# Expert 0's first layers: routing items, slot writes, turns, gate copies and zero blocks placed anew

## Chip, cores and metric

One core of a Trainium2 chip. The metric is the device time of one execution in microseconds (us), as the median of several runs. Its engines have a queue each and run side by side: TensorE (PE: matrix products and transposes into PSUM), VectorE (DVE), ScalarE (ACT), GpSimd (POOL) and SyncE (SP, which issues DMA transfers).

## What is computed

A sliding-window attention over 8 batches of 576 positions (8 heads of 64), whose 4608 output rows of 512 go through a layer of 8 experts. A noisy gate picks two experts for each row:

```python
logits = x @ w_gate
noise_scale = np.log1p(np.exp(x @ w_noise))
noisy_logits = logits + noise_scale * noise
top2 = np.argpartition(-noisy_logits, 2, axis=1)[:, :2]
...
for e in range(E):
    for k in range(2):
        mask = top2[:, k] == e
        h = np.maximum(x[mask] @ w1[e], 0.0)
        out[mask] += top2_w[mask, k, None] * (h @ w2[e])
```

## The kernel before

**Attention.** A loop over j = 0 to 38 handles one block of 128 rows per step: scores(j), softmax, transposition of the probabilities, product with the values (pv, two steps later), normalisation (three steps later), store of the rows to DRAM (`X`). Every part is issued by hand at a fixed place of the step, so each engine's order of work is the order of the program. The scores of block j use one PSUM tile `ps_s` of two banks, the transposes one bank `ps_t`; one bank `ps_g` (`idle`, `G`) is shared by the gate logits (`VG`), the ranks and the slot sums (`SP`).

**Routing.** The 36 blocks are routed in five portions that end at j = 7, 14, 21, 27 and 36 (`ROUTE`). `route(c)` is a generator of some 45 small operations of DVE and ACT (noise, top two, running counts, then after a pause of six calls, `HOLD`, a rank by two small matmuls, then weights and positions). `drain(n)` issues the next n of them. At its end `route` appends the **slot steps** of its portion to the list `slots`: for each pair of blocks `at_tile` (DVE), `at_lane` (four comparisons with `lane`, on POOL in the loop and on DVE after it), `at_both` (POOL) and `place` (four bfloat16 matmuls into `SP`, and a DVE addition into `SLOT`). `drain_slots(n)` issues the next n. The lists of rows that each expert handles are made from `SLOT`.

**Expert 0 starts early.** Its rows are handled in three chunks of 384, 384 and 448. The first two hold only rows of the blocks before 14 and 27 (`EARLY`), so they don't need the last portion of the routing; the third does. Per chunk c: `gather(0, c)` fetches rows by an indirect DMA on POOL into `xg` (four buffers, used by `down` for its results too); a **gate copy** on DVE takes each tile's weights; `turn_first(c)` transposes them (f: four PE transposes; g: an ACT copy and a DVE subtraction, the high and the low part); `up_first(c)` has 32 steps, f = 0 to 7 by k = 0 to 3, of three matmuls each, and after k = 3 an eviction (ACT L818, DVE L819); `down_first(c)` has 24 or 32 steps, three or four tiles q by f = 0 to 7, an ACT copy into `xg` and a scattered addition to the output (`add_rows`, L929 on POOL). Sixteen steps of up(0, 0) are issued in the steps j = 36 to 38 of the loop (`ahead`), the other sixteen (f = 4 to 7) after it. I write up00, down00, up01, down01, up02 for the stages, f5k2 for a step of an up, q1f3 for one of a down.

**Side work.** `spread(main, total, *parts)` issues the items of each part between the steps of a stage; a part (a, b, items) lies evenly over the shares a to b of it. Beside up00 and down00 lie: the split of w2 into high and low parts (`split_w2`, ACT L242 and DVE L234), the fifth portion of the routing, its slot steps, the turns of the next chunk, and `zero_out`, 38 transfers of 256 KB on SP's queue that clear the output before anything is added to it. `catch_up` makes sure that chunk 1's gather has been issued. `settle` and a `drain_slots` of everything stand in up01 ahead of the list of the third chunk (`first_list(2)`) and its gather.

Of the kernel before, what the change touches and what calls it, by code (L numbers as in the profile page):

```python
# [8 lines left out]
F32 = mybir.dt.float32  # L9
F32R = mybir.dt.float32r  # L10
BF = mybir.dt.bfloat16
# [3 lines left out]
OP = mybir.AluOpType  # L15
# [23 lines left out]
TURN = 33  # L39
# [7 lines left out]
ZFROM, ZEACH, ZUP = 32, 3, 8  # L47
# [40 lines left out]
def tile_kernel(ctx, tc, qT, kT, vx, vT, wgx, noise, w1, w2, out):  # L88
# [336 lines left out]
    lane = consts.tile([128, 128], F32)  # L425
# [73 lines left out]
    def route(c):  # L499
# [20 lines left out]
        d, ra = new("d"), new("ra")  # L520
# [6 lines left out]
        y = new("y")  # L527
# [3 lines left out]
        for c2 in range(2):  # L531
            t, r1 = new("t1"), new("r1", [128, n])
            yield lambda: nc.vector.tensor_reduce(mm[:, c2], y, op=OP.max, axis=AX.X)
            yield lambda: nc.vector.tensor_tensor(t, y, bc(mm[:, c2]), op=OP.is_ge)
            yield lambda: nc.vector.tensor_tensor(t, t, rev[:, None, :].to_broadcast(sh), op=OP.mult)
            yield lambda: nc.vector.tensor_reduce(r1, t, op=OP.max, axis=AX.X)
            yield lambda: nc.vector.tensor_tensor(oh[:, c2], t, bc(r1), op=OP.is_equal)
            if c2 == 0:
                yield lambda: nc.vector.copy_predicated(y, oh[:, 0].bitcast(U32),
                                                        low[:, :n * E].rearrange("p (a b) -> p a b", a=n))  # L540
# [44 lines left out]
        def at_lane(q, x):  # L585
            if x == 0:
                AB[q] = piece("ha", [128, 4, 128], BF, 2), piece("hb", [128, 4, 2, E * NQ], BF, 2)
            for k in range(2):
                (nc.gpsimd if j < NT else nc.vector).tensor_scalar(AB[q][0][:, 2 * x + k], lane, lo[:, q + x, k:k + 1], None, op0=OP.is_equal)
# [20 lines left out]
        last = None  # L610
        for q in range(0, n, 2):
            m = min(2, n - q)
            slots.append(lambda q=q, m=m: (at_tile(q, m), at_lane(q, 0)))
            slots.append(lambda q=q, m=m: m > 1 and at_lane(q, 1))
            slots.append(lambda q=q, m=m, f=last: (f and f(), at_both(q, m)))
            last = lambda q=q, m=m: place(q, m)
        slots.extend([lambda: None, last])
# [49 lines left out]
    GW = {}  # L667
    seen = {(0, c): j for c, j in enumerate(sorted(EARLY))}

    def gather(e, c):  # L670
# [9 lines left out]
        if e == 0:  # L680
            return [lambda q=q, m=m: whole(q, m) for q, m in tiles(e, c)] + [lambda: None] * 2 + [
                lambda q=q, m=m: gate_of(q, m) for q, m in tiles(e, c)]
# [17 lines left out]
    def turn_first(c):  # L700
# [7 lines left out]
        def f(q, m):  # L708
            y = cur[q] = turn_bank()[:, :KD * m].rearrange("p (k m) -> p k m", k=KD)
            for k in range(KD):  # L710
                nc.tensor.transpose(y[:, k], XG[0, c, q][:m, k * 128:k * 128 + 128], ident[:m, :m])

# [80 lines left out]
    def up_first(c):  # L793
# [5 lines left out]
        for f in (0, 4, 1, 5, 2, 6, 3, 7) if tail else range(KF):  # L799
# [11 lines left out]
            for k in range(KD):  # L811
                nc.tensor.matmul(p[:, :n], lhsT=w1h[:, k, fs], rhs=xh[:, k, :n], start=(k == 0), stop=False)
                nc.tensor.matmul(p[:, :n], lhsT=w1h[:, k, fs], rhs=xl[:, k, :n], start=False, stop=False)
                nc.tensor.matmul(p[:, :n], lhsT=w1l[:, k, fs], rhs=xh[:, k, :n], start=False, stop=(k == KD - 1))
                if k < KD - 1:
                    yield
            h, l, t = (x[f] for x in HH[e, c])
            nc.scalar.activation(h, p[:, :main], AF.Relu)  # L818
            nc.vector.scalar_tensor_tensor(l, p[:, :main], 0.0, h.bitcast(F32), op0=OP.max, op1=OP.subtract)  # L819
# [241 lines left out]
    for j in range(NT + 3):  # L1061
# [46 lines left out]
        drain_slots(2 if j >= DENSE else 1 + j % 2)  # L1108
# [18 lines left out]
    for n, (e, c) in enumerate(work):  # L1127
# [3 lines left out]
        if n == 0:  # L1131
            for w in split_w2():
                side += [lambda: (drain(3), drain_slots(1))] * 2 + [w]

            def catch_up():
                while (0, 1, 2) not in XG:
                    drain(1)
                    drain_slots(1)
        elif n == 1:
            pending.append(count())  # L1140
            side += [lambda: (drain(6), drain_slots(1))] * 12
            side += [settle, lambda: drain_slots(10 ** 6), lambda: [x() for x in first_list(2)], lambda: None]
        elif c == 0:
            parts.append((0.55, 1.0, split_w2()))
        if nxt and n:
            rows_of = gather(*nxt)
            if n < 2:
                side += rows_of + [lambda: None] * 2
            else:
                parts.append((0.0, 0.65, rows_of))  # L1150
# [5 lines left out]
        parts.append((0.0, 1.0, side))  # L1156
        if n == 0:
            parts.append((0.0, 0.8, [zero_out] * ZUP))
# [4 lines left out]
        if e == 0:  # L1163
            parts = [(0.7, 1.0, side) if nxt[0] == 0 else (0.05, 0.85, side)]
# [8 lines left out]
        if n == 1:  # L1173
            load_w1(1)
            parts.append((0.0, 0.6, list(other_lists())))
        if n == 0:
            parts.append((0.0, 1.0, [lambda: (drain(3), drain_slots(1))] * 29))
            parts.append((0.68, 0.69, [catch_up]))
            parts.append((0.0, 0.6, [zero_out] * len(blank)))
# [121 lines left out]
```

## Time and profile before

| | us |
|---|---|
| median of 3 runs (1045.77 to 1054.15) | 1047.35 |
| the profiled execution, its own time | 1048.88 |
| its span, first to last instruction | 1047.1 |

The profile gives the busy time of each engine, what ended each idle time, and the clock granted to PE (PEclk: 1.00 is 2.4 GHz, 0.50 is 1.2 GHz). Matmuls are pipelined, so that a busy PE need not be a fast one, and a matmul's duration is longer than its distance to the next. Attention ends, and the experts begin, at about 200 us of the span; the third chunk's down ends at 332 us, and seven experts of two chunks each follow.

### The profile page before, as it was taken

The numbers are of one execution on the slowest core, as the hardware profiler recorded it, in microseconds if no ns is written. First come the engines' busy times: TensorE is split into PE (matmuls) and PEld (weight loads), VectorE is DVE, ScalarE is ACT, GpSimd is POOL, SyncE is SP. The second block draws the span as 40 slices with busy tenths as digits, with TensorE's granted clock in tenths as the row PEclk, the third lists the DMA queues.
The fourth block names the chain that finished last, engine by engine and source line by source line (L and its number), as shares of the span: only waits on it lengthen the run. The fifth ranks groups of instructions, "written<-read, shape, count | busy, mean of one in ns | idle before, by whom it ended". The sixth has DMA issues, their size and how long they took to land.

```text
span 1047.1 us, 22033 instructions
## 1 busy us (share of the span) xinstructions
PE 985.3 (94%) x8433; PEld 881.9 (84%) x8433; DVE 708.9 (68%) x1804; ACT 522.2 (50%) x1305; POOL 336.9 (32%) x465
## 2 busy tenths in 40 slices
PE   9787878789999999999999999999999999999995
PEld 8776767677888998989898989898989898989894
DVE  5688888675177667776877687668666766686630
ACT  4885665441145545554554546355534554455430
POOL 5446555314233141323132313232322323141302
PEclk9998998899999999999999999999999999999998
DMA  9987888676175854685467546762776376557304
GB/s 335 365 273 219 255 242 283 212 226 184 38 158 132 225 92 92 158 218 111 81 181 185 124 65 197 171 144 40 220 153 143 48 226 138 136 105 180 46 1 53
DMA packets 107235, 168.94 MB, mean 161 GB/s; under 512 B 13360, under 2 KB 57648, under 8 KB 105328
## 3 DMA queue, kind: packets, MB, share of 16 engines
q1 hardware_dynamic: 89968, 126.96, 40.0%
q0 software_dynamic: 17152, 40.48, 22.1%
q8 instruction: 68, 1.11, 0.5%
q14 instruction: 47, 0.39, 0.1%
HBM read 110.08 MB, written 57.32 MB: 160 GB/s over the span
## 4 chain that ended last, share of the span: by engine, by line
PE 79%; DVE 10%; ACT 4%; issue 3%; POOL 2%; DMA 1%; SPq 0%; POOLq 0%; ACTq 0%; DVEq 0%
PE ps_d L996 8%; PE ps_d L995 8%; PE ps_d L997 8%; PE ps_z L851 6%; PE ps_z L853 5%; PE ps_z L852 5%; PE ps_o L376 3%; PE ps_v L851 3%; PE ps_y L996 2%; PE ps_y L997 2%; PE ps_y L995 2%; PE ps_v L853 2%; PE ps_v L852 2%; PE ps_y L851 2%; PE ps_y L853 2%
## 5 line engine op out<-in xcount | busy, mean ns | idle before, releaser
L929 POOL DMA_INDIRECT out_dram<-xg,los x70 | 110.4, 1578 | 400.0 <-ACT xg L1008 364.9
L996 PE MATMUL ps_d<-w2l,hb 128*128 128x512 f32 x392 | 152.9, 390 | 0.0
L995 PE MATMUL ps_d<-w2h,hb 128*128 128x512 f32 x392 | 152.8, 390 | 0.0
L997 PE MATMUL ps_d<-w2h,hb 128*128 128x512 f32 x392 | 152.6, 389 | 0.0
L863 ACT ACTIVATE hb<-tq 128x288 fp32r<-128x288 f32 (+1 forms) x168 | 77.1, 459 | 144.2 <-DVE tq L882 139.1
L882 DVE TENSOR_TENSOR tq<-ps_z,tq 128x288 f32<-128x288 f32 (+1 forms) x168 | 79.3, 472 | 87.7 <-PE ps_z L853 83.6
L851 PE MATMUL ps_z<-xh,WH 128*128 128x288 f32 (+1 forms) x448 | 137.3, 306 | 0.9
L853 PE MATMUL ps_z<-xh,WL 128*128 128x288 f32 (+1 forms) x448 | 135.0, 301 | 0.0
L852 PE MATMUL ps_z<-xl,WH 128*128 128x288 f32 (+1 forms) x448 | 134.9, 301 | 0.0
L867 DVE SCALAR_TENSOR_TENSOR hb<-tq,hb 128x320 fp32r<-128x320 f32 (+2 forms) x168 | 75.7, 451 | 37.6 <-ACT hb L863 34.8
L675 POOL DMA_INDIRECT xg<-xrows,lxs x70 | 70.5, 1006 | 85.9 <-DMA xs<-xg 36.0
L851 PEld LDWEIGHTS ps_z<-xh,WH 128*128 128x128 f32 x448 | 84.1, 188 | 5.6 <-DVE tq L882 3.8
L997 PEld LDWEIGHTS ps_d<-w2h,hb 128*128 128x128 f32 x392 | 73.6, 188 | 15.5
L995 PEld LDWEIGHTS ps_d<-w2h,hb 128*128 128x128 f32 x392 | 73.6, 188 | 14.1
L996 PEld LDWEIGHTS ps_d<-w2l,hb 128*128 128x128 f32 x392 | 73.6, 188 | 13.8
L852 PEld LDWEIGHTS ps_z<-xl,WH 128*128 128x128 f32 x448 | 84.1, 188 | 1.1
L853 PEld LDWEIGHTS ps_z<-xh,WL 128*128 128x128 f32 x448 | 84.1, 188 | 0.0
L395 ACT ACTIVATE x<-ps_o,r 128x80 f32<-128x80 f32 x288 | 67.0, 348 | 15.0 <-DVE r L387 14.9
L234 DVE TENSOR_TENSOR WL<-ws,WH 128x512 fp32r<-128x512 f32 x112 | 67.1, 614 | 3.7 <-ACT WH L242 3.4
L758 ACT ACTIVATE xh<-tq 128x512 fp32r<-128x512 f32 (+1 forms) x70 | 42.6, 609 | 51.0 <-DVE tq L754 48.9
L341 POOL TENSOR_TENSOR t<-t,mx 128x512 f32<-128x512 f32 x36 | 38.0, 1056 | 92.2 <-DVE mx L340 72.2
L376 PE MATMUL ps_o<-vw,pt 64*64 64x85 f32 x2176 | 56.0, 250 | 12.0 <-issue 7.6
(242 smaller groups left out, 2436.3 us busy)
## 6 DMA issues: line engine op xcount, KB each, us to landing
ws<-in_w_dram SPq DMA_DIRECT2D x14, 2048.0 KB
xs<-xg SPq DMA_DIRECT2D x63, 256.0 KB
vw<-in_vx_dram SPq DMA_DIRECT2D x36, 272.0 KB
out_dram<-zero SPq DMA_DIRECT2D x38, 256.0 KB
qc<-in_qT_dram SPq DMA_DIRECT2D x36, 256.0 KB
KW<-in_kT_dram SPq DMA_DIRECT2D x36, 256.0 KB
vt<-in_vT_dram SPq DMA_DIRECT2D x36, 256.0 KB
xrows<-x SPq DMA_DIRECT2D x36, 256.0 KB
```

What stands on the lines that cost most here:

```text
L376: nc.tensor.matmul(PO[j][u * 64:u * 64 + 64, a, g * 2 + x, :], lhsT=pt[pa, w, u * 2 + g, x * 64:x * 64 + 64], rhs=v[pa, (i + w) % 2, :, u, ...
L675: nc.gpsimd.indirect_dma_start(out=XG[e, c, q][:m], out_offset=None, in_=X[:DUMP + seen.get((e, c), NT) * 128], in_offset=bass.IndirectOff ...
L851: nc.tensor.matmul(p[:, :n], lhsT=WH[:, a, k, w], rhs=xh[:, b, k, :n], start=first and k == 0, stop=False, **free)
L852: nc.tensor.matmul(p[:, :n], lhsT=WH[:, a, k, w], rhs=xl[:, b, k, :n], start=False, stop=False, **free)
L853: nc.tensor.matmul(p[:, :n], lhsT=WL[:, a, k, w], rhs=xh[:, b, k, :n], start=False, stop=(k == 1), **free)
L863: nc.scalar.activation(hh[:, f, a:b], src, AF.Relu)
L867: nc.vector.scalar_tensor_tensor(hl[:, f, a:m], src[:, :m - a], 0.0, hh[:, f, a:m].bitcast(F32), op0=OP.max, op1=OP.subtract)
L882: nc.vector.tensor_tensor(t, a[:, :n], t, op=OP.add)
L929: s = nc.gpsimd.indirect_dma_start(out=out[:(2 + seen.get((e, c), NT)) * 128], out_offset=bass.IndirectOffsetOnAxis(ap=LT[e, c][1][q][:m], ...
L995: nc.tensor.matmul(p, lhsT=h, rhs=w2h[:, f, :], **a)
L996: nc.tensor.matmul(p, lhsT=h, rhs=w2l[:, f, :], start=False, stop=False)
L997: nc.tensor.matmul(p, lhsT=l, rhs=w2h[:, f, :], **b)
```

## The change

- The second `drain_slots` of a loop step issues 4 slot steps for j = 36 to 38 (2 before).
- `place` is put off: it is issued at the start of a later slot step, after the `at_both` of the pair that follows, so that two pairs are under way; `ha` has three buffers. Three temporaries of `route` share others' space.
- `lane` is bfloat16 (float32 before).
- The turns of chunk 0 start at j = 32 (33 before).
- The gate copies of expert 0 are issued with the transposes (`turn_first`'s f) instead of behind the gathers.
- The matmuls of up00's f = 1 are declared independent of the evictions of f = 0 (they use the two banks of one PSUM tile).
- up00 no longer drains the routing: beside it lie the w2 split and nine slot steps. down00 drains 2 items a call, 25 calls (3 items and a slot step, 29 calls, before), six slot steps, and the turns from 0.66 to 0.98 (0.7 to 1.0). The zero blocks of both stages go to up01 (eight) and down01.
- up01 gets twenty calls of one routing item and one slot step over 0 to 0.64, and `settle`, `first_list(2)` and the gather after 0.66.
- The turns of chunk 2 lie over 0.4 to 0.9 of down01 (0.7 to 1.0).

```diff
-TURN = 33
+TURN = 32
...
-    lane = consts.tile([128, 128], F32)
+    lane = consts.tile([128, 128], BF)
...
-        last = None
+        owed = []
+
+        def earlier(most):
+            if len(owed) > most:
+                place(*owed.pop(0))
         for q in range(0, n, 2):
             m = min(2, n - q)
-            slots.append(lambda q=q, m=m: (at_tile(q, m), at_lane(q, 0)))
+            slots.append(lambda q=q, m=m: (earlier(1), at_tile(q, m), at_lane(q, 0)))
             slots.append(lambda q=q, m=m: m > 1 and at_lane(q, 1))
-            slots.append(lambda q=q, m=m, f=last: (f and f(), at_both(q, m)))
-            last = lambda q=q, m=m: place(q, m)
-        slots.extend([lambda: None, last])
+            slots.append(lambda q=q, m=m: (at_both(q, m), owed.append((q, m))))
+        slots.extend([lambda: earlier(1), lambda: None, lambda: earlier(0)])
...
         if e == 0:
-            return [lambda q=q, m=m: whole(q, m) for q, m in tiles(e, c)] + [lambda: None] * 2 + [
-                lambda q=q, m=m: gate_of(q, m) for q, m in tiles(e, c)]
+            gate_first[c] = gate_of
+            return [lambda q=q, m=m: whole(q, m) for q, m in tiles(e, c)]
...
                 nc.tensor.transpose(y[:, k], XG[0, c, q][:m, k * 128:k * 128 + 128], ident[:m, :m])
+            gate_first[c](q, m)
...
+                if c == 0 and f == 1:
+                    for x in (m1, m2, m3):
+                        for y in evicted:
+                            tc.declare_no_dep(x.ins, y.ins, reason="another bank")
...
-        drain_slots(2 if j >= DENSE else 1 + j % 2)
+        drain_slots(4 if j >= NT else 2 if j >= DENSE else 1 + j % 2)
...
         if n == 0:
-            for w in split_w2():
-                side += [lambda: (drain(3), drain_slots(1))] * 2 + [w]
+            side += split_w2()
+            parts.append((0.0, 1.0, [lambda: drain_slots(1)] * 9))
...
-            side += [lambda: (drain(6), drain_slots(1))] * 12
-            side += [settle, lambda: drain_slots(10 ** 6), lambda: [x() for x in first_list(2)], lambda: None]
+            parts.append((0.0, 0.64, [lambda: (drain(1), drain_slots(1))] * 20))
+            parts.append((0.0, 0.9, [zero_out] * 8))
+            side += [settle, lambda: drain_slots(10 ** 6), lambda: [x() for x in first_list(2)]]
...
-                side += rows_of + [lambda: None] * 2
+                side += [lambda: None] * 2 + rows_of
...
-        parts.append((0.0, 1.0, side))
-        if n == 0:
-            parts.append((0.0, 0.8, [zero_out] * ZUP))
+        parts.append((0.66 if n == 1 else 0.0, 1.0, side))
...
-            parts = [(0.7, 1.0, side) if nxt[0] == 0 else (0.05, 0.85, side)]
+            parts = [((0.66, 0.98) if n == 0 else (0.4, 0.9) if n == 1 else (0.05, 0.85)) + (side,)]
...
+            parts.append((0.0, 0.4, [zero_out] * len(blank)))
         if n == 0:
-            parts.append((0.0, 1.0, [lambda: (drain(3), drain_slots(1))] * 29))
-            parts.append((0.68, 0.69, [catch_up]))
-            parts.append((0.0, 0.6, [zero_out] * len(blank)))
+            parts.append((0.0, 1.0, [lambda: drain(2)] * 25))
+            parts.append((0.0, 0.6, [lambda: drain_slots(1)] * 6))
+            parts.append((0.64, 0.65, [catch_up]))
```

## Rows read from the trace of the kernel before

**Rows 1.** Windows by stage: us, PE, PEld, DVE, ACT, POOL busy, clock, DMA, GB/s.

```profile
168.79:199.55 30.76, 22.98 (x461) 19.98 (x461) 24.41 (x64) 16.80 (x57) 18.25 (x23) 0.83 0.81 261
199.55:215.78 16.23, 14.77 (x192) 12.84 (x193) 7.79 (x25) 5.63 (x21) 3.99 (x4) 0.89 0.69 223
215.78:228.89 13.11, 9.89 (x54) 9.24 (x52) 10.32 (x40) 8.03 (x24) 2.99 (x3) 0.94 0.76 245
228.89:255.29 26.40, 22.50 (x104) 17.15 (x103) 17.50 (x51) 4.17 (x8) 9.61 (x10) 0.90 0.66 195
255.29:272.35 17.06, 17.06 (x99) 16.61 (x98) 6.14 (x20) 4.13 (x8) 5.52 (x6) 1.00 0.34 72
272.35:291.99 19.64, 18.54 (x89) 14.74 (x88) 3.18 (x9) 4.46 (x9) 3.34 (x5) 1.00 0.22 27
332.43:1047.10 714.67, 702.15 (x3977) 632.45 (x3975) 475.53 (x1168) 346.45 (x745) 196.80 (x273) 0.99 0.57 130
```

**Rows 2.** PE's waits, 170 to 345: us in total, times, longest.

```profile
PE ps_g L287 <- DVE SLOT L609: 4.1, 2, 2.5
PE ps_g L606 <- POOL xc L600: 3.9, 2, 2.9
...
PE ps_z L812 <- DVE hb L819: 1.5, 1, 1.5
...
PE ps_z L812 <- ACT xh L715: 1.1, 1, 1.1
```

**Rows 3.** Timeline of PE, 190 to 209: start, us, instruction, idle and releaser.

```profile
190.56 0.42 PE L606 MATMUL ps_g<-xc 128*128 128x160 bf16 x2 [1.52 <-DVE ebase L466]
...
198.21 0.66 PE L711 MATMUL ps_t<-ident,xg 128*128 128x128 f32 x4 [0.48 <-DVE pt L358]
...
199.55 0.44 PE L812 MATMUL ps_s<-xh,WH 128*128 128x384 f32 x1 [0.69 <-ACT xh L715]
...
206.96 0.44 PE L812 MATMUL ps_s<-xh,WH 128*128 128x384 f32 x1 [1.17 <-DVE WL L819]
...
208.12 0.45 PE L606 MATMUL ps_g<-xc 128*128 128x160 bf16 x4
...
208.36 0.42 PE L812 MATMUL ps_s<-xh,WH 128*128 128x384 f32 x1
```

**Rows 4.** Timeline, one pair's slot steps on DVE and POOL in down00.

```profile
237.03 0.48 DVE L594 TENSOR_TENSOR xc<-tl,xc 128x320 bf16<-128x320 f32 x1
...
237.43 1.86 DVE L589 TENSOR_SCALAR xc<-lane,xc 128x128 bf16<-128x128 f32 x4
...
237.65 1.37 POOL L600 TENSOR_TENSOR xc<-xc,mul 128x640 bf16<-128x640 bf16 x1 [0.82 <-DVE xc L594]
```

**Rows 5.** DVE's groups by line, 215.78 to 272.35: busy us, mean ns, idle.

```profile
L819 DVE SCALAR_TENSOR_TENSOR hb<-ps_z,hb 128x384 fp32r<-128x384 f32 x11 | 6.1, 555 | 8.3 <-ACT hb L818 6.7 <-issue 1.5
L234 DVE TENSOR_TENSOR w2l<-ws,w2h 128x512 fp32r<-128x512 f32 x8 | 5.4, 684 | 0.1
...
L609 DVE TENSOR_TENSOR SLOT<-SLOT,ps_g 128x160 f32<-128x160 f32 x6 | 1.9, 314 | 1.4 <-PE ps_g L606 1.4
```

**Rows 6.** The lane comparisons: duration ns min/median/max, first and last start.

```profile
L589 DVE TENSOR_SCALAR xc<-lane,xc x26: 274/278/1282, 201.3 to 246.6; 128x128 bf16<-128x128 f32 x26
```

**Rows 7.** Windows of PE's clock, columns as in rows 1.

```profile
222.00:227.00 5.00, 1.80 (x9) 1.20 (x8) 4.58 (x19) 2.55 (x6) 0.65 (x1) 1.00 0.97 329
227.25:230.65 3.40, 3.40 (x11) 3.01 (x11) 3.40 (x11) 0.00 (x0) 0.00 (x0) 0.51 0.50 175
...
241.00:244.30 3.30, 2.28 (x16) 1.80 (x16) 0.84 (x3) 0.00 (x0) 2.75 (x2) 1.00 1.05 346
...
200.00:203.40 3.40, 3.12 (x41) 2.69 (x45) 1.39 (x6) 1.00 (x5) 2.17 (x2) 0.50 0.91 273
```

**Rows 8.** The page, part 6: DMA issues of whole run, KB each.

```profile
ws<-in_w_dram SPq DMA_DIRECT2D x14, 2048.0 KB
...
out_dram<-zero SPq DMA_DIRECT2D x38, 256.0 KB
```

More of the change, by code (lines that the diff above doesn't have):

```diff
@@ L45 @@
 WARM = 4
-ZFROM, ZEACH, ZUP = 32, 3, 8
+ZFROM, ZEACH = 32, 3
 HOLD = 6
@@ L519, in route @@
         yield lambda: nc.scalar.activation(l, a, AF.Ln)
-        d, ra = new("d"), new("ra")
+        d, ra = new("d"), new("az")
         yield lambda: nc.vector.scalar_tensor_tensor(d, a, -1.0, u, op0=OP.add, op1=OP.subtract)
@@ L526, in route @@
         yield lambda: nc.vector.tensor_tensor(l, l, noise_sb[:, j0:j1, :], op=OP.mult)
-        y = new("y")
+        y = new("u")
         yield lambda: nc.vector.tensor_tensor(y, lg, l, op=OP.add)
@@ L531, in route @@
         for c2 in range(2):
-            t, r1 = new("t1"), new("r1", [128, n])
+            t, r1 = new("a"), new("r1", [128, n])
             yield lambda: nc.vector.tensor_reduce(mm[:, c2], y, op=OP.max, axis=AX.X)
@@ L586, in at_lane @@
             if x == 0:
-                AB[q] = piece("ha", [128, 4, 128], BF, 2), piece("hb", [128, 4, 2, E * NQ], BF, 2)
+                AB[q] = piece("ha", [128, 4, 128], BF, 3), piece("hb", [128, 4, 2, E * NQ], BF, 2)
             for k in range(2):
@@ L665, in other_lists @@
         return lists(slice(1, E), slice(0, NQ), "s")
-    GW = {}
+    GW, gate_first = {}, {}
     seen = {(0, c): j for c, j in enumerate(sorted(EARLY))}
@@ L811, in up_first @@
             for k in range(KD):
-                nc.tensor.matmul(p[:, :n], lhsT=w1h[:, k, fs], rhs=xh[:, k, :n], start=(k == 0), stop=False)
-                nc.tensor.matmul(p[:, :n], lhsT=w1h[:, k, fs], rhs=xl[:, k, :n], start=False, stop=False)
-                nc.tensor.matmul(p[:, :n], lhsT=w1l[:, k, fs], rhs=xh[:, k, :n], start=False, stop=(k == KD - 1))
+                m1 = nc.tensor.matmul(p[:, :n], lhsT=w1h[:, k, fs], rhs=xh[:, k, :n], start=(k == 0), stop=False)
+                m2 = nc.tensor.matmul(p[:, :n], lhsT=w1h[:, k, fs], rhs=xl[:, k, :n], start=False, stop=False)
+                m3 = nc.tensor.matmul(p[:, :n], lhsT=w1l[:, k, fs], rhs=xh[:, k, :n], start=False, stop=(k == KD - 1))
+                if c == 0 and f == 1:
+                    for x in (m1, m2, m3):
+                        for y in evicted:
+                            tc.declare_no_dep(x.ins, y.ins, reason="another bank")
                 if k < KD - 1:
@@ L817, in up_first @@
             h, l, t = (x[f] for x in HH[e, c])
-            nc.scalar.activation(h, p[:, :main], AF.Relu)
-            nc.vector.scalar_tensor_tensor(l, p[:, :main], 0.0, h.bitcast(F32), op0=OP.max, op1=OP.subtract)
+            evicted = [nc.scalar.activation(h, p[:, :main], AF.Relu),
+                       nc.vector.scalar_tensor_tensor(l, p[:, :main], 0.0, h.bitcast(F32), op0=OP.max, op1=OP.subtract)]
             if tail:
```

## Prediction, made before the change was run

> **What bounds the kernel now.** I read the windows by stage first. From 332.43 us on, PE is busy for 702 of 715 us at a clock of 0.99: nothing of the change acts there, and whatever is won ahead of it arrives at the end in full. The loss lies ahead: the end of attention and the stages of expert 0 up to 291.99 us [rows 1]. Two of those show what a stage costs when nothing holds PE up. up01 takes 17.06 us for 32 steps with PE busy throughout: 0.53 a step. down01 takes 19.64 us with 18.54 busy, for 24 steps and four turn pieces. Beside them up00's last 16 steps take 13.11 us (PE busy 9.89) and down00's 24 steps 26.40 us (22.50, at a clock of 0.90) [rows 1]. Then PE's waits: in up00 it waits 1.5 us for DVE's eviction (L819), in down00 for POOL's product (L600) ahead of a `place` [rows 2]. DVE is busy for 10.32 of up00's 13.11 us, on route(4), the w2 split and evictions in one queue [rows 1]. Last the clock: after the 5 us from 222 in which PE worked 1.80 us, it has 0.51 for 3.4 us; after 3.3 us with 2.28 of work it has 1.00 [rows 7].
>
> **The change part by part.** I counted in both orders between which steps each routing item and slot step is issued.
>
> *End of attention.* Before, at j = 34, `place` waits 1.52 us for the reservation of chunk 1 (ebase), its matmuls take 0.42, and scores(35) stands behind them; with place put off, no place lies there: -1.9. At j = 35 no turn is left: the wait of its transposes (0.48), they themselves (0.66) and up00's wait for their ACT copy (0.69) go: -1.8 [rows 3]. The turn that now starts at j = 32 adds there a DVE subtraction of 128x512 (as L234, 0.68 [rows 5]) and a transposition that stands ahead of scores(33); DVE is busy 24.41 of 30.76 us in j = 32 to 35 [rows 1], so a part of it is hidden: +0.3 (0 to 0.7). The wait of up00's f = 1 for the eviction of f = 0 (1.17 [rows 3]) is declared away. But at j = 36 there now stand two places close behind each other; the second needs the DVE addition of the first, and that stands on DVE behind the mask of block 35 and the gate reduction, so PE meets DVE's queue a few matmuls later: 0 (-1.2 to +0.6). That the logits no longer stand right behind a place (4.1 us of waits, L287 [rows 2]) I count as nothing, because at j = 32 the turn's transposes now wait there for the mask. Sum **-3.4**; bounds: 0, if the half clock of 200 to 203.4 [rows 7] returns and DVE hides the rest, and -7 with those 4.1 us.
>
> *up00.* The 24 DVE and ACT items of route(4) and the rank's matmuls leave. Left on DVE are eight w2 parts of 0.68 (5.5) and four evictions of 0.56 (2.2) [rows 5]: 7.7 us beside 16 steps of 0.53, 8.5. That just fits, and an eviction may be two f late since three banks rotate. 8.5 and 0.1 against 13.11: **-4.5** (bounds: 0, were DVE as late as before, and -4.6). No zero block of SP stands beside it any more, and chunk 1's gather is issued some steps earlier; both only help.
>
> *down00.* The nineteenth call of two items issues the rank, at q2f2, two tiles behind the last running count; DVE has nothing else there but turns. The five places, which PE waited for, leave for up01. down01's busy 18.54 is the pattern [rows 1]: one turn piece less, two rank matmuls more, so 18.5 against 26.40: **-7.9** (bounds -7 to -8.3). Where the stall goes is the next part.
>
> *up01.* From f1k0 to f5k2 it takes the slot steps of route(4), five places among them, and `count`. The price is DVE's. On POOL and DVE a pair goes like this: the comparison L594 starts at 237.03, POOL's L600 begins as it ends and runs 1.37 us, and the four lane comparisons last until 239.29, 1.86 us, though one takes 0.274 alone; one of each pair is stretched, up to 1282 ns, while POOL runs [rows 4, 6]. A pair holds DVE for 2.26 us. Four pairs 9.0, the single block an estimate of half, 1.1; four additions L609 of 0.31, 1.2; four evictions of 0.56, 2.2 [rows 5]; `count`, out of what DVE does in up01 besides eight evictions (6.14 - 4.5 [rows 1]), 1.4: together 14.9 us. DVE can begin once the eviction of f0 is through, 3.4 us after the start (four steps, ACT's copy of 0.5, 0.56, 0.3 for the latencies), and is done at 18.3. PE would stand at the last place after 23 steps and four places: a place takes 0.24 (208.12 to 208.36 [rows 3]), so 12.2 + 1.0 = 13.2. The put-off place gives each pair four steps, 2.1 us, and DVE alone needs 2.26 and an addition: PE waits 5.1 us over the five places. With their own 1.2: +6.3. PE then works for about two thirds of that stretch, near the 2.28 of 3.3 us after which the clock stayed up [rows 7], so I add 1.0, a part of the 1.7 that one half-clock stretch of 3.4 us takes: **+7.3** (bounds: +1.2, without any wait, and +11.4, with three such stretches that no wait hides).
>
> The lane operand in bfloat16 shortens the comparison a little or not at all; no row has that form, so I leave 0.274. The Trainium skill (VectorE: DVE Perf Modes, What auto-detection actually checks) has a 16-bit single-source operation in SBUF run four elements a cycle instead of two, an estimate of 33 ns less on 128 elements, 0.6 us over eighteen; by it the sum would be 0.6 lower. The same skill (SBUF — State Buffer, Who interferes with whom) has both modes take the port pair that GpSimd uses, so the stretched comparison would stay; no run here shows either yet.
>
> *down01 and zero blocks.* The turns of chunk 2 end three steps before up02: its wait of 1.1 us for the ACT copy [rows 2] goes, **-1.1** (bounds 0 and -1.1). The zero blocks, seventeen of 256 KB, and w1's 2048 KB [rows 8] now stand on SP behind the DMA of the weights of route(4), late in down00. They are hidden by up01, where DMA is at 0.34 of its time [rows 1]; the added rows of chunk 1 need the first eight of them some 20 us later. The next turn's list is made at f5k3 rather than f4k0, and its gather ends before down01: hidden by up01's last five steps and down01's first nine.
>
> Sum: -3.4 - 4.5 - 7.9 + 7.3 - 1.1 = -9.6 us. Against the profiled execution's own 1048.88 that gives 1039.3; its span is 1.8 less, which is left as it is. The profiled one lies 1.5 above the median of the runs, 1047.35, so in terms of the median: **1037.8**.
>
> **The rivals.**
>
> *DVE does not bind up01.* If POOL's product and the lane comparisons fall less on each other than in rows 4, or DVE comes early into up01, up01 costs +1.2 instead of +7.3: 1031.7. For it: the third pair's comparisons in down00 ran while POOL was at something else, and PE has four steps a pair. Against: DVE's 14.9 us against PE's 9.8 between the same two steps.
>
> *The clock falls in up01.* With a wait of a microsecond at each place the clock sinks for three stretches, and the end of attention keeps the one it has (1.7): +11.4 instead of +7.3 and -1.7 instead of -3.4, in all -3.8: 1043.6. For it: after 1.80 us of work in 5 it fell; against: after 2.28 in 3.3 it did not [rows 7].
>
> *The DMA backlog makes chunk 2's rows late, and the kernel slower.* Place: SP's queue from the end of down00, 17 x 256 KB and 2048 KB and then the gather's 1 MB on the same sixteen engines, 7.4 MB. At the 195 GB/s of down00's row [rows 1] that is 38 us, about when the last turn of down01 wants its tile (24.4 us of up01 and 18 steps of 0.71: 37). The turns stand in PE's queue and would hold it. It decides from 9.6 us of such waits on, 7.4 MB in 47 us, 157 GB/s; at 130 GB/s, 57 us, it costs 20: 1057.8. Against: 245 and 261 GB/s in busier windows [rows 1].
>
> That the change does not do what it says: the rows moved are in an order written by hand, so only their effect can be missing; up00's part at 0 would be in the range.
>
> **How the numbers follow.** The forecast 0.45 (1034 to 1041.5), DVE not binding 0.22, clock 0.28, slower 0.05. The time is the forecast's. The range runs from 1030, below the first rival, to 1044.5, above the second; it leaves out the slower case and the tails of the bounds, under 2 in 10. About 1% is what a measurement of this kernel can tell from no change, 1036.9 and 1057.8. Faster by more: the first rival and two fifths of the forecast, 0.22 + 0.18 = 0.40. Slower by more: half and more of the last case, 0.04. Within: 0.56.
>
> **What would show each step.** In the windows by stage of the changed kernel: j = 32 to 36 about 3 us shorter; up00's last sixteen steps near 8.6 us with no wait for L819; down00 near 18.5 us, no L606 in it; up01 near 24 us, with waits of L606 for DVE's lane comparisons or POOL; up02 without its 1.1. It is wrong if up01 takes under 20 us, if up00 still waits for DVE, or if transposes (L711) in down01 wait for a DMA.

## The result, and the profile after

The changed kernel takes 1037.43 us (median; 1034.4 to 1038.6) beside 1050.75 us for the kernel before on the same chip: ratio 0.9864, 95% interval 0.9834 to 0.9894. Its profiled execution took 1036.78 us with a span of 1035.1. The forecast was 1037.8 us, counted from the earlier median of 1047.35. Against the runs beside it the gain is 13.3 us where 9.6 were forecast; the median of the kernel before is 3.4 us higher in these runs than the one that the forecast was counted from, and the two differences nearly cancel. That the time came out nearer than the steps did is luck.

The windows by stage of the kernel after (us; PE, PEld, DVE, ACT, POOL busy with instructions; PE's clock; DMA share; GB/s). The lines are up00's first four f, its last four (16 steps), down00, up01, down01, up02, down02, and the rest:

```profile
197.61:212.24 14.63, 13.07 (x194) 11.85 (x194) 8.99 (x27) 6.79 (x25) 7.57 (x9) 1.00 1.01 354
212.24:221.86 9.62, 8.60 (x49) 8.28 (x49) 4.79 (x11) 7.43 (x22) 2.88 (x4) 1.00 0.51 156
221.86:239.91 18.05, 18.05 (x88) 14.59 (x87) 12.40 (x46) 4.75 (x11) 3.30 (x4) 1.00 0.25 33
239.91:260.99 21.08, 19.16 (x117) 17.58 (x115) 14.86 (x48) 4.13 (x8) 9.57 (x8) 1.00 1.04 330
260.99:279.45 18.46, 18.46 (x90) 14.94 (x89) 3.88 (x12) 3.83 (x7) 5.23 (x7) 1.00 0.38 76
279.45:300.17 20.72, 19.88 (x97) 17.88 (x96) 15.89 (x37) 9.58 (x24) 8.27 (x12) 1.00 0.59 154
300.17:320.57 20.40, 20.40 (x90) 16.36 (x88) 17.55 (x47) 10.55 (x22) 4.95 (x6) 1.00 0.64 161
320.57:1035.10 714.53, 702.27 (x3977) 632.39 (x3975) 475.45 (x1168) 346.51 (x745) 198.97 (x273) 0.99 0.57 130
```

Beside [rows 1]: up00 starts at 197.61 instead of 199.55, its first four f take 1.60 us less, the last four 3.49 less, down00 8.35 less with PE busy throughout, up01 4.02 more, down01 1.18 less; up02 and down02 (20.20 and 20.24 before) give 0.68 back; the rest is 0.14 shorter. Together 12.0 us, the difference of the spans.

PE's waits of the kernel after, 195 to 345 us (us in total, times, longest):

```profile
PE ps_g L606 <- DVE SLOT L609: 3.5, 4, 1.6
PE ps_z L816 <- DVE hb L827: 1.0, 1, 1.0
PE ps_z L816 <- DVE hb L830: 0.8, 1, 0.8
```

POOL's product and ACT's turn copies of [rows 2] are gone. The wait for L827 lies in up00, that for L830 in up02. One of the four L606 waits lies at j = 36, where a second place follows the first (1.56 us, foreseen and priced at nothing); three lie in up01, on PE's timeline (start, us, instruction, idle and releaser):

```profile
246.03 0.46 PE L606 MATMUL ps_g<-xc 128*128 128x160 bf16 x4
249.14 0.45 PE L606 MATMUL ps_g<-xc 128*128 128x160 bf16 x4 [1.03 <-DVE SLOT L609]
251.43 0.45 PE L606 MATMUL ps_g<-xc 128*128 128x160 bf16 x4 [0.21 <-DVE SLOT L609]
254.19 0.45 PE L606 MATMUL ps_g<-xc 128*128 128x160 bf16 x4 [0.68 <-DVE SLOT L609]
```

### The profile page after: what moved, and what is told of

Same layout as the page of the kernel before. It is cut to its first block, busy times and chain, and to the rows that moved or that the text cites. A ratio compares the mean times of both kernels' runs of the same rounds, so it can differ in the third digit from the quotient of the medians.

```text
span 1035.1 us, 22027 instructions
## 1 busy us (share of the span) xinstructions
PE 978.1 (94%) x8433; PEld 875.7 (85%) x8433; DVE 707.2 (68%) x1800; ACT 521.6 (50%) x1305; POOL 341.5 (33%) x469
## 4 chain that ended last, share of the span: by engine, by line
PE 77%; DVE 11%; DMA 4%; ACT 3%; issue 3%; POOL 1%; SPq 0%; POOLq 0%; ACTq 0%; DVEq 0%
PE ps_d L1004 8%; PE ps_d L1003 8%; PE ps_d L1005 8%; PE ps_z L859 6%; PE ps_z L861 6%; PE ps_z L860 6%; PE ps_v L859 3%; PE ps_v L861 2%; PE ps_v L860 2%; PE ps_y L1005 2%; PE ps_y L1004 2%; PE ps_y L1003 2%; PE ps_y L860 2%; PE ps_y L859 2%; PE ps_y L861 2%
```

## Experiments on the spread of route(4)

All edits below are made on the kernel after. The ratio is always to the kernel before on the same chip; the stages come from the windows of each run's trace.

**e_drains** puts the routing items and the slot steps of route(4) back into up00 and down00.

```
-            side += split_w2()
-            parts.append((0.0, 1.0, [lambda: drain_slots(1)] * 9))
+            for w in split_w2():
+                side += [lambda: (drain(3), drain_slots(1))] * 2 + [w]
...
-            parts.append((0.0, 1.0, [lambda: drain(2)] * 25))
-            parts.append((0.0, 0.6, [lambda: drain_slots(1)] * 6))
+            parts.append((0.0, 1.0, [lambda: (drain(3), drain_slots(1))] * 29))
```

> The changed kernel with route(4)'s items and slot steps drained in up00 and down00 as before (3 items and a slot step a call); place stays put off. Theory: what the change wins in up00 and down00 is that DVE's queue there is free of route(4), and a part is paid in up01. Then up00's last sixteen steps go from 9.6 us to about 13, down00 from 18.05 to 22 to 26 with waits of L606 again, up01 from 21.1 to 17.2; together 5 to 9 us more than the changed kernel. Rival: that place is put off is what frees PE, wherever the routing lies: down00 under 20, together at most 3 us more.

Measured: 1042.11 us, ratio 0.992 (0.9887 to 0.9953). Its windows, up00's last 16 steps, down00 and up01:

```profile
213.69:227.28 13.59, 10.00 (x51) 9.36 (x51) 10.08 (x34) 8.21 (x24) 2.79 (x3) 0.89 0.38 116
227.28:250.92 23.64, 21.59 (x103) 16.72 (x103) 18.26 (x54) 3.95 (x8) 9.32 (x10) 0.92 0.84 267
250.92:268.07 17.15, 17.15 (x98) 16.63 (x97) 5.68 (x17) 4.13 (x8) 3.29 (x3) 1.00 0.33 71
```

up00 and up01 have the times of the kernel before again, down00 two thirds of its loss, with waits of L606 of 1.3 and 0.7 us and a clock below 1.00 in both early stages. The three stages sum to 54.38 us against 48.75 after: the spread is worth 5.6 us. This part of the theory held.

**e_place** takes the put-off of the place back (the place is issued just ahead of the next pair's `at_both`).

```
...
-            slots.append(lambda q=q, m=m: (at_both(q, m), owed.append((q, m))))
-        slots.extend([lambda: earlier(1), lambda: None, lambda: earlier(0)])
+            slots.append(lambda q=q, m=m, f=last: (f and f(), at_both(q, m)))
+            last = lambda q=q, m=m: place(q, m)
+        slots.extend([lambda: None, last])
```

> The changed kernel with place issued as before, ahead of the next pair's product. Theory: DVE sets up01, so place asked for a step sooner waits that step longer and the stage ends nearly the same: up01 from 21.1 to 21 to 22.5 us; at the end of attention the logits wait for the slot sum again and place for the reservation, 1 to 3 us more. Rival: the put-off alone made the places cheap: up01 at 24 or more.

Measured: 1036.80 us, ratio 0.9892 (0.9844 to 0.994). up01 takes 21.60 us instead of 21.08; up00 starts at 194.79, earlier than in the kernel after. The put-off is worth 0.5 us in up01 and by itself nothing that the total shows.

**e_act** gives the products of route(4) from POOL (L600) to ACT, as eight scaled copies a pair.

```
+            if c == len(ROUTE) - 2:
+                for x in range(2 * m):
+                    for v in range(2):
+                        nc.scalar.activation(AB[q][1][:, x, v], AB[q, 1][:, x], AF.Copy,
+                                             scale=mul[:, q + x // 2, x % 2, v:v + 1])
+                return
```

> The changed kernel with the last portion's products (at_both) made by ACT, 16 scaled copies of 80 columns for two pairs of four, eight a pair, instead of one POOL product a pair. Theory: it is POOL's product that stretches DVE's lane comparisons in up01 (two comparisons 0.94 to 1.15 us instead of 0.40). With POOL idle there no comparison is stretched, the waits of L606 (1.9 us) fall under 0.5 and up01 goes from 21.1 to about 19.3 us, unless ACT's eight copies, an estimate of 2 us a pair, now come last. Rival: the chain from tile to place is too long for four steps, whichever engine multiplies: waits of L606 stay at 1.9 us or grow, up01 21 to 23.

Measured: 1039.52 us, ratio 0.9898 (0.9851 to 0.9945); up01 22.91 us. The lane comparisons of up01 (duration ns min/median/max, first and last start), in the kernel after:

```profile
L589 DVE TENSOR_SCALAR xc<-lane,xc x18: 235/242/1251, 244.4 to 254.5; 128x128 bf16<-128x128 bf16 x18
```

And in e_act:

```profile
L589 DVE TENSOR_SCALAR xc<-lane,xc x18: 232/245/249, 242.7 to 253.4; 128x128 bf16<-128x128 bf16 x18
```

With no product on POOL the stretched ones are gone: the longest takes 249 ns instead of 1251. On DVE's timeline four comparisons take 1.73 us beside the product and 0.72 without it; that POOL's product stretches them is shown. up01 is slower all the same by 1.83 us, and the eight copies of a pair now come last (PE waits 1.4 us in five places for ACT's L602). PE's idle time in the stage grows by only 0.46 us; the other 1.37 counts as busy, which no run explains. POOL's 1.3 us with a stretched DVE is the cheaper of the two.

**e_lane** puts the lane operand back to float32 (`consts.tile([128, 128], F32)`).

> Only the lane operand is float32 again, and with it the comparisons of DVE. Four pairs and a single block in up01 have 18 comparisons; at 31 to 39 ns each that is 0.6 to 0.7 us. If DVE paces up01 (my theory), the stage takes 21.6 to 21.8 us instead of 21.08. If POOL's product paces it (a rival: the comparisons end with it), the stage stays at 21.1. In both, the stretched comparison of each pair stays over 1.2 us, and the total moves by less than a measurement can tell: 1037.4 to 1038.1.

Measured: 1037.58 us, ratio 0.9853 (0.9803 to 0.9903); up01 21.68 us instead of 21.08. Its lane comparisons in up01:

```profile
L589 DVE TENSOR_SCALAR xc<-lane,xc x18: 268/272/1274, 245.8 to 256.4; 128x128 bf16<-128x128 f32 x18
```

One is 30 ns longer at the median, eighteen of them 0.54 us, and up01 grows by 0.60: with the steps at this spacing DVE's queue paces up01. The total can't tell it.

**e_lanefirst** issues a pair's lane comparisons ahead of its tile comparison, so that they end before POOL starts on the product of that pair.

```
-            slots.append(lambda q=q, m=m: (earlier(1), at_tile(q, m), at_lane(q, 0)))
-            slots.append(lambda q=q, m=m: m > 1 and at_lane(q, 1))
+            slots.append(lambda q=q, m=m: (earlier(1), at_lane(q, 0)))
+            slots.append(lambda q=q, m=m: (m > 1 and at_lane(q, 1), at_tile(q, m)))
```

> The changed kernel with at_tile issued behind the four lane comparisons of its pair instead of ahead of them. POOL's product can begin only once at_tile is done, so that the pair's comparisons run before it. Theory: the stretch of the comparisons (1.7 us for four in up01, 0.72 when POOL is idle) is DVE time that PE waits for; four then take about 0.75 us in most pairs and up01 falls from 21.1 to between 19.3 and 20.3 us. Rival: PE waits for the addition into SLOT, which stands behind evictions, whatever the comparisons take: up01 20.8 to 21.3.

Measured: 1035.07 us, ratio 0.9877 (0.9839 to 0.9915); up01 21.44 us, no shorter. Its lane comparisons in up01:

```profile
L589 DVE TENSOR_SCALAR xc<-lane,xc x18: 232/236/1328, 240.6 to 251.0; 128x128 bf16<-128x128 bf16 x18
```

The longest still takes 1328 ns, and DVE's work in the stage is 15.1 us, no less than in the kernel after: the product now falls on the next pair's comparisons, and once on `count`'s last DVE step. The edit moved the stretch and did not remove it, so that it can't tell what a removal would be worth. In up01 PE now waits for L589 (0.9 us in two waits), for that step of `count` (L641, 0.8) and for POOL's product (0.6) instead of L609.

**e_wide** gives the slot steps more of up01: they reach to 0.85 of the stage instead of 0.64, and the list and rows of the next turn come behind.

```
-            parts.append((0.0, 0.64, [lambda: (drain(1), drain_slots(1))] * 20))
+            parts.append((0.0, 0.85, [lambda: (drain(1), drain_slots(1))] * 20))
...
-        parts.append((0.66 if n == 1 else 0.0, 1.0, side))
+        parts.append((0.87 if n == 1 else 0.0, 1.0, side))
```

> The changed kernel with up01's twenty calls of a routing item and a slot step over 0 to 0.85 of the stage instead of 0 to 0.64, and settle, chunk 2's list and gather after 0.87. Theory: DVE has 12 us of work from count to the last addition; over 0.64 of the stage PE has 11 us, over 0.85 it has 14.5, so PE's waits vanish but for a few tenths: up01 from 21.1 to 18.5 to 19.3 us, and down01 stays at 18.46. Rival: the rows of chunk 2 then come too late: transposes in down01 wait for their DMA and down01 takes 20 or more, so nothing is left of it.

Measured: 1032.89 us, ratio 0.986 (0.9807 to 0.9914). Its windows of up01 and down01:

```profile
239.54:258.34 18.80, 18.73 (x117) 17.52 (x115) 14.95 (x48) 4.13 (x8) 8.02 (x7) 1.00 1.03 326
258.34:276.80 18.46, 18.46 (x90) 14.94 (x89) 3.89 (x12) 3.83 (x7) 6.89 (x9) 1.00 0.52 121
```

DVE has the same 14.9 us of work as in the kernel after, but PE's waits of L606 in up01 are gone: its idle time falls from 1.92 to 0.07 us and its busy time by 0.43, 2.28 in all, and down01 still meets its rows in time. So DVE isn't too slow for up01; the steps stood too close. 1.74 us are left above the 17.06 of [rows 1]. Most of it is the five places: by PE's timeline one takes 0.25 us (247.15 to 247.40), and the matmul behind it 0.26 to its successor (247.40 to 247.66) where others take 0.17, about 1.5 us for all five. The rest is not traced; the matmul of `count` stood in up01 before, too.

The median is the lowest here, but so is that of the kernel before on this chip (1047.68 us). By the ratio, 0.986 against 0.9864, the total doesn't show the 2.28 us.

**e_zero** puts the zero blocks back to where they were issued before (up00 and down00, on SP).

```
-            parts.append((0.0, 0.9, [zero_out] * 8))
...
+        if n == 0:
+            parts.append((0.0, 0.8, [zero_out] * 8))
...
-            parts.append((0.0, 0.4, [zero_out] * len(blank)))
...
+            parts.append((0.0, 0.6, [zero_out] * len(blank)))
```

> The changed kernel with the last seventeen zero blocks issued beside up00 and down00 as before instead of up01 and down01. Theory: no engine waits for them in either place, so every stage stays within 0.3 us and the median within 1.5 us. Rival: beside up00 they compete with the store of attention's last tile, for which ACT's copy of f4 waits, and with chunk 1's gather: up00's last sixteen steps 10.5 or more instead of 9.6, transposes in down00 wait, the median 2 us more.

Measured: 1036.70 us, ratio 0.9899 (0.9856 to 0.9942). up01's DMA share falls from 1.04 to 0.43 and the stages stay (9.65, 18.04, 21.10, 18.46 us). The DMA at full share in up01 costs nothing: the mechanism that I had for a slower kernel is not at work.

## Experiments on up00, up02 and the end of attention

**e_spare** lays all eight f of chunk 0's relu outputs in the spare part of the weight tiles instead of four.

```
-    spare = [x[:, :4 * 384].rearrange("p (q n) -> p q n", q=4) for x in flat]
+    spare = [x[:, :8 * 384].rearrange("p (q n) -> p q n", q=8) for x in flat]
...
-            if c == 0 and f < 4:
+            if c == 0:
...
-                if f == (0 if c else 4):
+                if f == 0:
```

It tests the one wait that up00 kept. In the kernel after, PE's f = 7 stands for 1.02 us, and before it ACT's first eviction to the ordinary memory waits for a store from that memory (ACT's timeline):

```profile
218.53 0.49 ACT L826 ACTIVATE hb<-ps_z 128x384 fp32r<-128x384 f32 x1 [1.24 <-DMA xrows<-x]
```

> The changed kernel with all eight f of chunk 0's hidden values in the spare part of the weight tiles, instead of f = 4 to 7 in hb, which lies where attention's last output tile lay. Theory: in up00 ACT's copy of f4 waited for the DMA that stores that tile, and with it the DVE eviction for which PE waited 1.02 us at f7k0; without it up00's last sixteen steps take 8.6 instead of 9.6 us and all later starts come 1.0 us sooner. Rival: DVE's w2 split (5.5 us) and evictions hold it anyway: 9.3 or more.

Measured: 1036.43 us, ratio 0.9869 (0.9829 to 0.9909). The window of up00's last 16 steps:

```profile
213.21:221.56 8.35, 8.35 (x50) 8.35 (x49) 4.86 (x11) 7.40 (x23) 2.88 (x4) 1.00 0.56 173
```

9.62 becomes 8.35 with PE busy throughout. The cause, the memory where attention's last tile was on its way to DRAM, is shown; the total is too coarse for 1.3 us. The wait depends on the timing, too: in e_attall, below, the same memory is used and the steps take 8.40.

**e_best2** joins e_spare and e_wide and starts the first part of up02's split of w1 later.

```
-                      [(a, b, nextw[q]) for q, a, b in ((0, 0.02, 0.12), (1, 0.14, 0.3), (2, 0.33, 0.5), (4, 0.34, 0.5),
+                      [(a, b, nextw[q]) for q, a, b in ((0, 0.08, 0.14), (1, 0.14, 0.3), (2, 0.33, 0.5), (4, 0.34, 0.5),
...
```

It comes from DVE's timeline of the kernel after in up02, where the sums of the split hold the eviction behind them:

```profile
280.94 1.03 DVE L234 TENSOR_TENSOR WL<-ws,WH 128x512 fp32r<-128x512 f32 x2 [4.09 <-ACT WH L242]
282.00 1.80 DVE L264 TENSOR_TENSOR ws<-ws 128x256 f32<-128x256 f32 x4
283.72 0.55 DVE L827 SCALAR_TENSOR_TENSOR hb<-ps_z,hb 128x384 fp32r<-128x384 f32 x1
284.56 0.23 DVE L830 SCALAR_TENSOR_TENSOR hb<-ps_z,hb 128x64 fp32r<-128x64 f32 x1 [0.29 <-ACT hb L829]
```

> Three edits on the kernel after, each seen in a stage of its own. (1) All eight f of chunk 0 lie in the spare part of the weight tiles: up00's last 16 steps 8.35 us instead of 9.62, as in e_spare. (2) The slot steps of route(4) reach to 0.85 of up01 and the next turn's rows come behind them: up01 18.8 us instead of 21.08, as in e_wide. (3) The first part of the split of w1 in up02 begins at 0.08 of the stage instead of 0.02, behind the eviction of f = 0. By my reading of up02 (four sums of 1.80 us stand on DVE ahead of that eviction, because a wait of PE for ACT that once lay ahead of them is gone) up02's wait of 0.8 for L830 goes and the stage takes 20.0 to 20.2 us instead of 20.72. The rival reading is that the split is too much for up02 wherever it stands: then the wait only moves to a later f and the stage keeps 20.7. Sum by the first: -1.3 -2.3 -0.6 = -4.2 on 1037.4, 1033 us; by the second 1033.8.

Measured: 1033.94 us, ratio 0.9823 (0.9772 to 0.9874). up00's steps take 8.35 and up01 18.80, as in the single runs; up02 grows to 21.39. PE's only wait from 276 to 298 us:

```profile
PE ps_z L816 <- DVE hb L830: 1.5, 1, 1.5
```

The eviction of f = 0 now goes ahead, but 4.0 us of split, from 280.50 to 284.52 us on DVE, stand ahead of that of f = 1: the wait moved and nearly doubled. The rival reading had it move; that it grows neither had. The earlier place of the split is better. Of the pair after against e_best2 the stages show 3.5 us less in up00 and up01 and 0.7 more in up02; e_best2 has the lowest ratio of all runs, but its interval overlaps that of the kernel after.

**e_att** undoes three of the attention edits: the turn starts at j = 33, two slot steps a block also at the end, the gate reductions between the slot steps; the declared no-dependence of f = 1 goes too. **e_attall** is e_att, e_place and e_lane in one; only the scratch names of `route` and the three buffers of `ha` stay as in the kernel after. **e_before** is the kernel before once more. The edit of e_att, hunk by hunk:

```
-TURN = 32
+TURN = 33
...
-            return [lambda q=q, m=m: whole(q, m) for q, m in tiles(e, c)]
+            return [lambda q=q, m=m: whole(q, m) for q, m in tiles(e, c)] + [lambda: None] * 2 + [
+                lambda q=q, m=m: gate_of(q, m) for q, m in tiles(e, c)]
...
-            gate_first[c](q, m)
...
-                if c == 0 and f == 1:
+                if False:
...
-        drain_slots(4 if j >= NT else 2 if j >= DENSE else 1 + j % 2)
+        drain_slots(2 if j >= DENSE else 1 + j % 2)
```

> The changed kernel with the parts that act in the attention loop undone: turns from j = 33, two slot steps a call for j = 36 to 38, f = 1 dependent on the eviction of f = 0, gate copies behind the gathers; place put off and all of expert 0's staging as changed. Theory: the change won 3.5 us there, so the first matmul of up00 starts about 2 us later and f0 to f3 take 16 instead of 14.6 us; the median is 2 to 4 us above the changed kernel's. Rival: four executions with the changed order of attention begin up00 anywhere from 195 to 199 us, so this part is the loop's own scatter: f0 to f3 under 15 us, the median within 1.5 us of the changed kernel's.

> The whole of the attention edits undone, all else as after: the turn from j = 33, two slot steps a block, one at j = 36, the gate reductions between the slot steps, the place in its old position, the lane operand in float32. My prediction gave the edits 3.4 us: 1.9 ahead of up00 and 1.5 in its first four f. If that is right, the time from the scores of the block that starts near 152 us to up00's first matmul goes from 42 to 46 (seen in eight runs of the new order) to 48, the first four f from 14.6 to 16.2, and the total rises by about 3.5 to 1041 us. The rival, from e_att (turn, steps and gates undone, and no later start of up00 than in the others): only the turn part is real, the first four f take 15.8 to 16.2, the rest lies within the scatter of attention, and the total rises by 1.2 to 1.6, to 1039.

> The kernel before once more, for the scatter of attention's end: its first profile has up00's first matmul at 199.55 us, and 48.4 us from the scores near 151 us to it. Runs of the new order have 42.1 to 46.0 there. If the old order is really slower there, this profile has 47 us or more again; if it was scatter, 42 to 46. From up00's first matmul on, the stages should repeat the first profile within 0.3 us each.

Measured: e_att 1035.64 us, ratio 0.9881 (0.9841 to 0.9922), up00's first four f 15.77 us; e_attall 1044.07 us, ratio 0.9933 (0.9899 to 0.9967), 6.6 us above the kernel after; e_before, run once, 1055.77, and its up00 starts at 207.12 instead of 199.55. Its stages from up00 on (first four f, last 16 steps, down00, up01) take 16.41, 12.38, 26.53 and 17.06 us beside 16.23, 13.11, 26.40 and 17.06 in [rows 1]: all but the second within the 0.3 that I had expected.

In e_att two waits of the kernel before are back in up00:

```profile
195.23 0.44 PE L816 MATMUL ps_s<-xh,WH 128*128 128x384 f32 x1 [0.69 <-ACT xh L719]
202.75 0.45 PE L816 MATMUL ps_s<-xh,WH 128*128 128x384 f32 x1 [1.17 <-DVE WL L827]
```

PE's idle time in the first four f is no longer for it, 1.46 us beside 1.56 in the kernel after, where the second place waits; the 1.14 us more lie in busy time, at a clock of 0.89 beside 1.00. The 6.6 us of e_attall are not those of attention alone: its up01 takes 22.44 us, 1.36 more than in the kernel after, where e_place and e_lane add 0.52 and 0.60.

So up00's start differs between two traces of one kernel by more than I wanted to read from it. A steadier measure is the stretch from the same row of scores (that at 151.12 us in the first trace of before) to the end of up00's first four f, with nearly the same count of PE rows in each. Its window in the first trace of the kernel before:

```profile
151.12:215.78 64.66, 53.05 (x978) 46.77 (x978) 44.92 (x127) 33.71 (x117) 30.03 (x35) 0.84 0.81 263
```

In e_before:

```profile
159.43:223.53 64.10, 51.98 (x978) 45.98 (x978) 44.32 (x127) 33.57 (x117) 29.91 (x35) 0.87 0.82 265
```

In e_attall:

```profile
156.65:219.75 63.10, 49.30 (x979) 42.78 (x978) 44.69 (x128) 33.49 (x117) 29.90 (x35) 0.92 0.83 269
```

In the kernel after:

```profile
153.20:212.24 59.04, 46.86 (x978) 41.48 (x978) 45.27 (x128) 33.34 (x116) 33.81 (x41) 0.94 0.87 286
```

In e_att:

```profile
152.41:211.00 58.59, 47.01 (x970) 41.32 (x970) 43.77 (x127) 33.43 (x116) 27.08 (x31) 0.94 0.87 290
```

And in e_place:

```profile
152.39:209.07 56.68, 44.97 (x978) 40.64 (x978) 43.23 (x127) 33.32 (x116) 32.29 (x40) 0.97 0.87 290
```

With the whole old order the stretch takes 63.1 to 64.7 us in three traces, otherwise 56.7 to 61.5 in eleven. The time in which PE stands, length less busy, is 12.5 us in the mean of the three and 11.6 in that of the eleven (12.18 in the kernel after, 11.61 in the first trace of before). PE's busy time is 51.4 us in the mean of the three and 46.9 in that of the eleven, for the same matmuls, at a granted clock of 0.84 to 0.92 and 0.91 to 0.97. So 4.5 of the 5.4 us lie in PE's busy time and 0.9 in waits. Busy time times granted clock is 43.4 to 45.4 us in all fourteen, 45.1 in the mean of the three and 44.1 in that of the eleven: an estimate from these means puts 3.4 of the 4.5 us down to the clock and leaves 1.1 without a cause. None of e_att, e_place and e_lane alone makes the stretch long. Why the clock falls less, and which edits it takes, stays open; e_drains and e_lane, at 0.92, have 60.53 and 61.54 us, so the two groups nearly meet.

The waits did move inside the stretch. From the scores of j = 32 to up00's first matmul (30.76 us, 22.98 of them busy, in [rows 1]), and from the row at 151.12 to the scores of j = 32, the first line before, the others after:

```profile
151.12:168.79 17.67, 15.30 (x325) 13.95 (x324) 12.72 (x40) 11.28 (x41) 7.79 (x9) 0.81 0.92 302
153.20:171.96 18.76, 13.28 (x329) 11.38 (x329) 15.47 (x40) 11.86 (x44) 12.99 (x16) 1.00 0.96 326
171.96:197.61 25.65, 20.51 (x460) 18.26 (x458) 20.81 (x64) 14.69 (x48) 13.25 (x17) 0.87 0.71 219
```

Behind the scores of j = 32 PE stands 2.6 us less than before (5.14 and 7.78), ahead of them 3.1 us more (5.48 and 2.37). In the means of the groups it is 3.3 less (4.9 in the eleven, 8.1 in the three) and 2.3 more (5.2 and 2.9).

## Why the prediction was right, step by step

**End of attention, -3.4.** The pair of traces gives -3.54 (1.94 at the start of up00, 1.60 in its first four f), but that number is luck: between the same rows the pair differs by 5.6 us, and from the scores of j = 32 to up00 by 5.1, where I had expected about 3. I added up waits that would go: ebase, the turn at j = 35, f = 1's eviction. These did go, and from the scores of j = 32 to up00 PE stands 2.6 us less in the pair. The step that failed is that little comes in their place. Over the whole stretch PE stood nearly as long as before, since places now wait behind ACT's copy of the logits, the longest of them just ahead of the scores of j = 32, and the second of the two places at j = 36 waits 1.56 us. The first is among PE's waits from 170 us on:

```profile
PE ps_g L606 <- ACT vw L293: 3.4, 3, 2.0
```

These waits come with the edits that e_att undoes, not with the put-off place: e_place has 5.4 us of them, e_att 0.7 and e_attall none.

Most of the shorter stretch went with the clock (0.50 in one part of it before, [rows 7]), which I had as a bound only; the 1.60 us of the first four f are PE's busy time alone, 14.77 and 13.07 us at clocks of 0.89 and 1.00. And the size is known less well than I wrote it: up00 starts between 194.2 and 199.1 us in the eleven traces that have the new order or a part of it, the stretch above is 5.4 us shorter in them, and the medians of e_attall and the kernel after lie 6.6 us apart.

**up00, -4.5; measured -3.5.** The cause was right: route(4) in DVE's queue; e_drains brings 13.6 us back. But by my own sign ("if up00 still waits for DVE") a step failed: PE still waits 1.02 us for a DVE eviction, and that is the missing 1.0. It is late because ACT's eviction waits for memory that attention's last x tile still occupied (e_spare), a wait that the trace of before doesn't have and that I put at nothing. The stage before took 13.11 us in one trace and 12.38 in e_before, so the gain is known to about 0.7 us.

**down00, -7.9; measured -8.35.** 18.05 us, no L606, PE without a gap at a clock of 1.00; before it had 0.90 [rows 1].

**up01, +7.3; measured +4.0.** The mechanism was right: DVE's lane comparisons beside POOL's product pace the places, and PE waits for L609. The term was mis-sized. I had 5.1 us of waits, 1.2 of places and 1.0 of clock; measured are 1.9 of waits, 2.1 more of PE work and no clock loss. Of the 2.1, about 1.5 are the places with the slower matmul behind each, where I had 1.2. The waits I had from 14.9 us of DVE work. One part of the error is that I had summed durations, while most rows start before the one ahead of them ends: in the lines below L594 takes 0.47 and its successor starts 0.40 later, and L609 takes 0.30 with its successor 0.23 later. DVE's timeline in up01, two stretches:

```profile
246.72 0.47 DVE L594 TENSOR_TENSOR xc<-tl,xc 128x320 bf16<-128x320 f32 x1
247.12 1.73 DVE L589 TENSOR_SCALAR xc<-lane,xc 128x128 bf16<-128x128 bf16 x4
248.78 0.30 DVE L609 TENSOR_TENSOR SLOT<-SLOT,ps_g 128x160 f32<-128x160 f32 x1
249.01 0.47 DVE L594 TENSOR_TENSOR xc<-tl,xc 128x320 bf16<-128x320 f32 x1
```

From the start of one L594 to that of L609 it takes 2.06 us, where I had 2.26 for a pair, and all of it from `count` on 12.0 us instead of 14.9. Counted from start to start, and without the rows of others between, the four pairs take 7.5 us instead of 9.0 (the bfloat16 lane is 0.5 of that, and two pairs are stretched less), the single block 0.57 instead of 1.1 (its comparisons are not stretched), and additions, evictions and `count` together 3.9 instead of 4.8, mostly by the overlap. With 12.0 in place of 14.9 my own sum closes: DVE starts 3.4 us into the stage, is done at 15.4, and PE, at 13.2, would wait 2.2 us; it waits 1.9. The overlap could have been read in [rows 4]: L594 there has 0.48, and the next row starts 0.40 later.

**The bfloat16 lane, priced at nothing.** A comparison takes 242 ns at the median instead of 272 in e_lane (30 less) and 278 in [rows 6]. My estimate from the rule of the Trainium skill (VectorE: DVE Perf Modes, What auto-detection actually checks), four elements a cycle instead of two, was 33 ns, and the trace agrees. The Trainium skill (SBUF — State Buffer, Who interferes with whom) also has such a mode share a port pair with GpSimd, one of them locking the other out: the longest comparison of 1251 ns beside POOL's product, and of 249 without one, agrees with that too.

**down01, -1.1; measured -1.18.** But 0.5 of it came back in up02, which I hadn't looked at. Before, up02's wait of 1.1 us for ACT [rows 2] gave ACT time to begin the split of w1 at 291.83 us, 0.16 ahead of up02's first matmul; now it begins at 280.28, 0.83 behind it, and the four sums of L264 meet the eviction of f = 0, and PE waits 0.8 for it. I read this from the starts; no run puts the old wait back alone. e_best2 shows that the place of the split, not the amount alone, sets this wait.

**The rivals.** That DVE doesn't bind up01 holds half: PE does wait for it, but e_wide shows that this lay in the spacing. The clock in up01 stayed at 1.00, against the second rival, though PE waited over 1 us at a place. That rival also took 1.7 us off the 3.4 of attention, which were waits and held no term for the clock. The backlog did not show: up01's DMA share went to 1.04, but down01 has no wait, and e_zero is no faster. That the range held is in part luck, errors of both signs: up01 3.3 us better and down00 0.4 better, against 1.0 in up00 and 0.7 in up02 and down02. The forecast had "within 1%" as likelier than "faster"; the measured 1.4% faster lies beyond it. In the pair of traces, 12.0 us where 9.6 were forecast, that is mostly those 3.3 us; the rest of the 13.3 lies between the profiled executions and the medians.

## What to carry to other kernels

Price a queue by the distance between the starts of successive rows, not by adding durations, and price a spread by how evenly its steps stand as well as by the engine's sum: e_wide made up01 2.3 us shorter, 1.9 of them waits, without taking any work out of DVE. For each wait that goes, look at which queue it had given time to, and read that stage too; here up02 grew by 0.5 us when down01 lost 1.2. And compare stretches between the same two rows of work in several traces before crediting an edit with a start time: PE's busy time and idle time, held apart, show whether waits moved it, and the granted clock beside the busy time how much may be the clock's.

## What the chip showed that I had not expected

Two traces of the same kernel (before and e_before) put up00's start at 199.55 and 207.12 us; all of the difference lies ahead of the stretch, whose first row starts at 151.12 and 159.43. Between the kernels before and after, 978 PE rows of the stretch took 53.05 us at a granted clock of 0.84 and 46.86 at 0.94, while PE's idle time was within 0.6 us. And a lane comparison on DVE, 249 ns at most without a POOL product, takes up to 1251 ns in the kernel after, where one of about 1.3 us falls on it.
